# Sigmoid attention and a token-mixing MLP on one core: the whole order of work planned anew, with fixed buffers taken in turn

## The chip, the cores and the metric

The kernel runs on one core of a Trainium2 chip. The metric is the device time of one execution in microseconds (us). A core has five engines that each work through their own list of instructions in order: TensorE (PE in the profile: matmuls; its weight loads are PEld), VectorE (DVE), ScalarE (ACT), GpSimd (POOL) and SyncE (SP, which here only issues DMA transfers). An instruction that waits for a semaphore holds up everything behind it on its own engine.

## What is computed

```python
# q, k, v: (8, 12, 448, 64) float32; 8 sequences, 12 heads
scores = scale * np.matmul(q, k.transpose(0, 1, 3, 2)) - np.log(S)
attn = 1.0 / (1.0 + np.exp(-scores))
attn_out = np.matmul(attn, v)
# x: the heads side by side, (8, 448, 768)
wq = x @ w_q                       # 768 -> 64
wk = x @ w_k                       # 768 -> 64
W_tok = scale * np.einsum('bsd,btd->bst', wq, wk)
mixed = np.einsum('bst,btd->bsd', W_tok, x)
out = np.maximum(mixed, 0.0) @ w_out     # 768 -> 768, float32
```

Matmuls run in bf16. The kernel never forms W_tok: it computes wk-transposed times x first (a 64x768 matrix per sequence, `tmp`) and then wq times that.

## The kernel before

The work is cut into 24 groups of four heads (n = 0 to 23), three to a sequence. For each group the kernel loads q, k and v (448 KB each, `load1`) in float32 on SyncE's queue into eight load buffers, casts them to bf16 (`cast1`), transposes q and k into a tile `qk` (`tr`), and then takes seven steps. Step i of a group computes the scores of 64 keys against all 448 queries for four heads with four 64x64 quarter matmuls (`scores`, L328), turns them through one sigmoid on ScalarE into a tile `at` (L333), and multiplies `at` with v, again four quarter matmuls accumulating over the seven steps (`values`, L350). After the seventh step VectorE copies the sum to `xt` (L359).

How q and k of a group get transposed differs by group and is one letter in the plan. Kinds a and q go through TensorE: matmuls against the identity (L246 or L238) and one or two copies from PSUM on VectorE (L302, L316). Kind c interleaves pairs in the cast (L201); six copies of 32 partitions on GpSimd (`arrange`, L163 to L169) put the blocks in place and two transposes of 128x448 on VectorE (L285) finish it. Kind r ("quadrants") does without GpSimd's copies: two transposes of 128x448 (L278) and four of 32x448 (`quadrants`, L254) on VectorE.

Per sequence the MLP follows: `tr_x` transposes `xt` back to token order `xn`, either as eight whole 128x128 matmuls (L372) or as 32 quarter ones (L388); `mlp_wqk` makes wq and wk (L425, or in quarters L413), `mlp_wkn` transposes wk, `mlp_tmp` makes `tmp`, `mlp_mix` the mixed tokens with a relu into `mx` (L480 on VectorE, L478 on ScalarE), and `out_pair`, `out_halves` and `out_chunk` multiply with w_out and store.

The order of all this is written out by hand as one string, `PLAN` (L134), read one letter at a time by the loop at L828. A letter emits one step (S scores, P values, x or X a transpose of xt, W, N, U, M, O for the MLP; the choice of letter sets the engine of a copy or the tiling). The list `BANKS` (L69) says, one entry for each use, which of the eight PSUM banks it takes. `ORDER` (L705) is the order of the loads and casts: a plain entry is cast on GpSimd, a dot means VectorE, a capital ScalarE. `pump_loads` (L728) issues a load when the buffer eight loads back has been cast; `pump` (L778) emits GpSimd's casts as soon as the tiles that they write are free. Tiles come from rotating pools. Filler letters F and f (L830, L835) emit matmuls on zeros that nothing reads.

Of the kernel before, what the change touches and what calls it, by code (L numbers as in the profile page):

```python
# [17 lines left out]
def kernel(  # L18
# [112 lines left out]
    TW = (1, 2,)  # L131
# [4 lines left out]
        "PSPPPPSSXWzSSwWWSWWXSNSSPPPrSsPPUSPPzSPSPSPCMPPPSPSqkSSMSXSM"
        "SCcPPPSPPxSPdPSOSwwrSSwwWWxSOSSOsOSNPPSPPzCPSPPSIISISIcPSPdP"
        "PSPS2SPPOOSxSUSPPSMPPPcSPPSdOwWwSSMWWWoSMPPSPPPP1SSPcdOQSxSO"
        "OSSNCSOOXcdSSOOSTSPPPSrPPCPSPPCPPSPPPSPSOwowSSSwsOzOxSwwWPSP"
        "MSPPPPRSScSdXXOXoSMSOoNSMPPSPcPPSPPSUdSOSMOSOMoPSPPcPPSPSdPw"  # L140
        "WXWSMSWWWXSSONOScTSOSOSOOdSPOSrOSPPPGPPSPPPSPPsPSPOSPOSOzSQS"
        "XPcPPSPPPSPOSOdSOSxOlLlSLlLPSPPPxPP2GSPOOScOmdOSOOSNO1SQSTPP"
        "PcS1PPSPOPSOSOQSMOSOSOdScOOSdOMSOmOP2PSPPxSPPP12SOSOSOSxOllL"
        "SllcSLPPPSPPPSPOOdSxSOOSOSOSONQSTPSPPPSPPPSPPPxPPmPPLxLlMlGL"
        "lOOyOoNIItIiIMimIiMOoOOOoOoOOOOOOOOOoOO"
# [787 lines left out]
```

## Time and profile before

| | |
|---|---|
| runs, us | 181.77, 180.97, 180.97 (median 180.97) |
| span of the profiled execution, first to last instruction | 180.1 us |
| instructions in it | 7907 |
| busy: TensorE matmul | 169.6 us, 94% |
| busy: VectorE | 145.6 us, 81% |
| busy: ScalarE | 159.0 us, 88% |
| busy: GpSimd | 121.4 us, 67% |
| granted TensorE clock | 1.000 |
| moved by DMA | 47.31 MB, mean 263 GB/s |

Busy shares are averages over the span; the engines wait for each other in different ways at its start, in its middle and after the last sigmoid, so the stages have to be read apart. In a timeline row the first number is the start in us from the span's start, the second the time until the last instruction of the row ends; matmuls are pipelined, so the distance from one start to the next says what one costs. Of a row with a bracket, the bracket is the idle time of the engine ahead of it and what ended it.

### The profile page before, as it was taken

What the parts mean: (1) busy time and instruction counts of PE and PEld (TensorE: products, weight loads), DVE (VectorE), ACT (ScalarE), POOL (GpSimd) and SP (SyncE); (2) the same over time, 40 slices, a digit from 0 to 9 for tenths busy, and PEclk for the clock granted to TensorE, in tenths of its full rate; (3) what the DMA queues carried; (4) which work ended last, traced back from release to release, by engine and by line L of the source; (5) the groups of instructions that cost most, each with busy time, mean ns of one, the idle gap of its engine ahead of it and who ended that gap; (6) DMA issues with size and microseconds to landing.
All of it is one profiled execution on the core that took longest, in us unless ns stands there. A gap on an engine that the chain in (4) does not pass through costs nothing.

```text
span 180.1 us, 7907 instructions
## 1 busy us (share of the span) xinstructions
PE 169.6 (94%) x3440; PEld 112.2 (62%) x3440; DVE 145.6 (81%) x227; ACT 159.0 (88%) x208; POOL 121.4 (67%) x166
## 2 busy tenths in 40 slices
PE   7698899889899999999999999999999999999990
PEld 3334445444575555445667786678887788888660
DVE  3578899997989896889999999979898886768351
ACT  4699999999899999999999999999999989976300
POOL 1028799689999999999999999979979910010000
PEclk9999999999999999999999999999999999999999
DMA  5999999999999998899998889987795523505876
GB/s 177 355 372 349 322 383 381 280 302 356 342 294 349 339 265 267 217 319 365 343 300 315 217 288 305 342 322 213 200 338 173 135 64 73 137 4 122 201 208 175
DMA packets 27475, 47.31 MB, mean 263 GB/s; under 512 B 3888, under 2 KB 23600, under 8 KB 27440
## 3 DMA queue, kind: packets, MB, share of 16 engines
q1 hardware_dynamic: 26160, 44.64, 78.0%
q0 software_dynamic: 800, 1.18, 3.6%
q10 hardware_dynamic: 480, 0.98, 1.5%
q8 instruction: 27, 0.44, 1.0%
q14 instruction: 8, 0.07, 0.1%
HBM read 35.78 MB, written 11.01 MB: 260 GB/s over the span
## 4 chain that ended last, share of the span: by engine, by line
PE 56%; POOL 16%; DMA 15%; DVE 5%; ACT 2%; issue 2%; SPq 1%; POOLq 0%
PE banks L539 15%; PE banks L350 10%; PE banks L328 10%; PE banks L620 8%; DMA q<-in_q_dram 6%; POOL qk L201 5%; DMA w<-in_moe_w_k_dram 4%; DMA k<-in_k_dram 3%; POOL qk L169 3%; DMA wout<-wout 2%; ACT at L333 2%; POOL v L218 2%; PE banks L579 2%; PE banks L413 2%; POOL swap L163 2%
## 5 line engine op out<-in xcount | busy, mean ns | idle before, releaser
L333 ACT ACTIVATE at<-banks 128x896 bf16<-128x896 f32 x168 | 140.0, 948 | 3.4 <-PE banks L328 3.0
L328 PE MATMUL banks<-qk 64*64 64x448 bf16 x672 | 62.2, 358 | 3.3 <-ACT at L333 1.6
L350 PE MATMUL banks<-at,v 64*64 64x448 bf16 x672 | 47.3, 351 | 0.8 <-ACT at L333 0.7
L328 PEld LDWEIGHTS <-qk 64*64 64x64 bf16 x672 | 25.9, 105 | 20.7 <-issue 13.2
L539 PE MATMUL banks<-wout,mx 64*64 64x384 bf16 x672 | 36.6, 323 | 0.0
L201 POOL CAST qk<-k 128x896 bf16<-128x896 f32 x19 | 22.8, 1199 | 10.6 <-DVE qk L302 9.7
L350 PEld LDWEIGHTS <-v 64*64 64x64 bf16 x672 | 23.2, 107 | 8.6 <-issue 1.7
L539 PEld LDWEIGHTS <-mx 64*64 64x64 bf16 x672 | 23.3, 107 | 4.5 <-issue 0.5
L359 DVE CAST xt<-banks 128x896 bf16<-128x896 f32 x22 | 23.8, 1083 | 2.3 <-PE banks L350 1.8
L620 PE MATMUL banks<-wout,mx 128*128 128x384 bf16 (+1 forms) x138 | 24.4, 320 | 0.0
L480 DVE TENSOR_SCALAR mx<-banks 128x1024 bf16<-128x1024 f32 (+3 forms) x22 | 21.3, 972 | 1.9 <-PE banks L493 0.7
L201 POOL CAST qk<-q 128x896 bf16<-128x896 f32 x17 | 20.4, 1198 | 2.6 <-DMA q<-in_q_dram 1.3
L218 POOL CAST v<-v 128x896 bf16<-128x896 f32 x22 | 20.6, 950 | 1.4 <-DMA v<-in_v_dram 0.4
L620 PEld LDWEIGHTS <-mx 128*128 128x128 bf16 x138 | 12.3, 98 | 9.8 <-issue 3.2
L285 DVE STREAM_TRANSPOSE qk<-qk 128x448 f32<-128x448 f32 x28 | 17.0, 627 | 0.4 <-POOL qk L166 0.3
L163 POOL COPY swap<-qk 32x448 uint32<-32x448 uint32 x28 | 15.5, 554 | 2.3 <-DVE qk L201 0.7
L166 POOL COPY qk<-qk 32x448 uint32<-32x448 uint32 x28 | 15.8, 566 | 1.6
L169 POOL COPY qk<-swap 32x448 uint32<-32x448 uint32 x28 | 15.8, 564 | 1.6
L254 DVE STREAM_TRANSPOSE qk<-qk 32x448 f32<-32x448 f32 x24 | 15.3, 636 | 0.6
L422 POOL COPY wq<-wqk 64x448 bf16<-64x448 bf16 x3 | 1.7, 555 | 15.7 <-DVE wqk L421 15.7
L653 DVE COPY o<-banks 128x384 f32<-128x384 f32 x12 | 6.6, 553 | 5.7 <-PE banks L620 5.3
L653 ACT COPY o<-banks 128x384 f32<-128x384 f32 x9 | 4.4, 490 | 7.1 <-PE banks L620 6.9
(91 smaller groups left out, 206.5 us busy)
## 6 DMA issues: line engine op xcount, KB each, us to landing
q<-in_q_dram SPq DMA_DIRECT2D x24, 448.0 KB, 6.6
v<-in_v_dram SPq DMA_DIRECT2D x24, 448.0 KB, 6.3
k<-in_k_dram SPq DMA_DIRECT2D x23, 448.0 KB, 7.0
out_dram<-o SPq DMA_DIRECT2D x50, 192.0 KB, 3.9
wout<-in_moe_w_out_dram POOLq DMA_DIRECT2D x2, 576.0 KB, 12.2
wout<-wout SPq DMA_DIRECT2D x12, 96.0 KB, 6.2
out_dram<-o ACTq DMA_DIRECT2D x4, 192.0 KB, 3.5
k<-in_k_dram SPq DMA_DIRECT2D x1, 256.0 KB, 5.6
```

The lines of the kernel that those rows point to most:

```text
L163: eng.tensor_copy(out=z[lo], in_=w[hi, 0])
L169: eng.tensor_copy(out=w[lo, 1], in_=z[lo])
L201: COPY[e](out=f[:, :, "qk".index(nm)].rearrange("p e i d y -> p e y i d"), in_=ld.pop((nm, n)),)
L218: COPY[e](out=t16.rearrange("p b i d -> p (b i d)"), in_=ld.pop((nm, n)).rearrange("p b x -> p (b x)"),)
L285: nc.vector.transpose(out=qk[n][:, t].rearrange("p t i n -> p (t i n)").bitcast(F32), in_=w)
L328: nc.tensor.matmul(sc[HALF[h], g, 0:S], qk[n][HALF[g], h, 1, i, :], qk[n][HALF[g], h, 0].rearrange("p i n -> p (i n)"), start=True, stop=True,
L333: inst = nc.scalar.activation(at, sc[:, :, 0:S], ACTF.Sigmoid, bias=attn_bias, scale=attn_scale)
L350: nc.tensor.matmul(ps[HALF[g], h, 0:S], ld["v16", n][HALF[h], g, i, :], ats[n, i][HALF[h], g, :], start=(i == 0), stop=(i == NI - 1),)
L359: read(fb, COPY[eng](out=xt(u, j)[:, :, 0:S], in_=ps[:, :, 0:S]))
L480: inst = nc.vector.tensor_scalar(dst, ps, moe_scale, 0.0, ALU.mult, ALU.max)
L539: nc.tensor.matmul(ps[HALF[x], y, 0:NB], mx[HALF[y], u, b, 64 * (i - 3 * y) : 64 * (i - 3 * y) + 64], wout16[HALF[y], slot(y, b), x * NB : ...
L620: nc.tensor.matmul(ps, mxs[w][:, 2 * S * c + m * P : 2 * S * c + (m + 1) * P], wout16[:, c, w0:w1], start=(c == 0), stop=(c == NC - 1),)
```

## The change

The change rewrites the plan, the order of loads and the choice of banks, and replaces the rotating pools by fixed buffers.

- Each entry of `PLAN` now carries its banks ("S23": scores in banks 2 and 3); the `BANKS` list is gone. There are 625 entries in place of 640. The six F and four f fillers are gone.
- `p_ld`, `p_c16`, `p_v16`, `p_qk`, `p_x`, `p_mx` and `p_o` become lists of fixed tiles, in the same numbers, taken in turn (`turn`, or by n modulo the count). A load takes any free buffer of the eight (`borrow`), and one that has been cast goes back to the list; before, the buffers went round in a ring.
- Casts: four are on VectorE (k1, k6, v10, v12) where there were seven (q1, k1, q2, q12, q22, k22, v22), none on ScalarE (v19 before), the others on GpSimd; v6 is loaded and cast in one go by GpSimd's own DMA (L225 after). v0 is now loaded ahead of k2.
- Kinds: five groups in quadrants (3, 4, 5, 8, 18) where there were six (2, 4, 5, 8, 13, 18); TensorE transposes groups 0, 1, 2 and 6 (before 0, 1, 3 and 6); the other 15 (before 14) are of kind c.
- `tr_x`: 18 groups in quarter matmuls and 6 in whole ones (before 14 and 10).
- Some copies change engine. TensorE's list changes its tiling 58 times, the one after the matmuls that warm it up among them (before 68).

The core of the diff (`PLAN` and `ORDER` cut to a line each; other lines that take a pool tile change in the same way as those shown):

```diff
-    p_ld = pool("ld", 8)
-    p_c16 = pool("c16", 2)
-    p_v16 = pool("v16", 4)
-    p_qk = pool("qk", 8)
...
+    lds = [singles.tile([P, 2 * RUN + PAD], F32, name=f"ld{n}") for n in range(8)]
+    v16s = [singles.tile([P, 2, NI, HD], BF16, name=f"v16{n}") for n in range(4)]
+    qks = [singles.tile([P, 2, 2, NI, NP], BF16, name=f"qk{n}") for n in range(8)]
...
+    def turn(nm, bufs):
+        turns[nm] = turns.get(nm, -1) + 1
+        return bufs[turns[nm] % len(bufs)]
+
+    def borrow(key):
+        held[key] = free.pop(0)
+        return held[key]
...
     PLAN = (
-        "ffSSSffKSSF11aSb1SFFrSFSFSSFSqSPPsPPSPzkPSPSPPPSxSrSsPPPPSPPS"
...
+        "S23 S45 K01 1 S67 S01 S23 a45 S01 b S23 S01 S45 S01 S45 q23 S01 p67 P k S45 P P r p R "
...
-        t = p_ld.tile([P, 2, NI * HD], F32, tag="ld", name=nm + "32")
+        t = halves(borrow((nm, n)))
...
-            qk[n] = p_qk.tile([P, 2, 2, NI, NP], BF16, tag="qk", name="qk")
+            qk[n] = qks[n % 8]
...
     ORDER = (
-        ".q1 .k1 k2 .q2 q3 v0 w2 k3 v1 k4 q4 v2 w0 k5 q5 w1 v3 W5 v4 q6 k6 w4 k7 v5 q7 v6 q8 k8 k9 "
...
+        "q1 .k1 v0 k2 q2 q3 k3 v1 k4 q4 v2 w0 v3 q5 v4 k5 w1 q6 w4 v5 .k6 q7 *v6 k7 q8 k8 q9 k9 "
...
-            if len(ring) >= 8 and ring[-8] not in cast:
+            if not free:
                 break
...
         cast.add((nm, n))
+        if (nm, n) in held:
+            free.append(held.pop((nm, n)))
         pump_loads()
...
-    for t in PLAN:
+    for t, b in PLAN:
+        assert not bank
+        if b:
+            bank.append(b)
```

Where the change moves instructions, first on VectorE, early, before the change: from the cast of group 2's q on. Here qk_283 and qk_429 are the casts of groups 2 and 4 that the transposes read, xt_111 to xt_113 the attention sums of groups 0 to 2.

```order
L201 CAST qk_283<-q_169 128x2x2x224
L278 STREAM_TRANSPOSE qk<-qk_283 128x448 x2
L254 STREAM_TRANSPOSE qk<-qk_283 32x448 x4
L316 COPY qk<-banks 128x2x2x448
L359 CAST xt_111<-banks 128x2x448
L401 COPY xn<-banks 128x2x4x128
L278 STREAM_TRANSPOSE qk<-qk_429 128x448 x2
L254 STREAM_TRANSPOSE qk<-qk_429 32x448 x2
L359 CAST xt_112<-banks 128x2x448
L359 CAST xt_113<-banks 128x2x448
L377 COPY xn<-banks 128x4x256
L254 STREAM_TRANSPOSE qk<-qk_429 32x448 x2
```

The same place on VectorE after the change (L290 and L266 are the transposes, L328 the copy of a group that TensorE transposed, L371 the xt cast, L413 and L389 the xn copies). qk_114, qk_115 and qk_116 are the transposed tiles of groups 2, 3 and 4.

```order
L328 COPY qk_114<-banks 128x2x2x448
L290 STREAM_TRANSPOSE qk_115<-qk_120 128x448 x2
L371 CAST xt_90<-banks 128x2x448
L266 STREAM_TRANSPOSE qk_115<-qk_120 32x448 x4
L413 COPY xn_126<-banks 128x2x4x128
L371 CAST xt_91<-banks 128x2x448
L290 STREAM_TRANSPOSE qk_116<-qk_121 128x448 x2
L266 STREAM_TRANSPOSE qk_116<-qk_121 32x448 x2
L371 CAST xt_92<-banks 128x2x448
L389 COPY xn_126<-banks 128x4x256
L266 STREAM_TRANSPOSE qk_116<-qk_121 32x448 x2
```

Group 2 has moved from VectorE's quadrants to TensorE, group 3 the other way. The six transposes that stood ahead of the copy of a TensorE group now stand behind one.

On ScalarE, in the last third, before the change (at is a sigmoid, v16 the bf16 form of v19, mx a relu, o an output copy):

```order
L333 ACTIVATE at4_99<-banks_88 128x896
L218 CAST v16_3054<-v32_2231 128x896
L478 ACTIVATE mx_2640<-banks_88 128x512
L333 ACTIVATE at5_100<-banks_88 128x896
L333 ACTIVATE at6_101<-banks_88 128x896
L478 ACTIVATE mx_2640<-banks_88 128x2x512
L333 ACTIVATE at7_102<-banks_88 128x896
L333 ACTIVATE at8_103<-banks_88 128x896
L333 ACTIVATE at9_104<-banks_88 128x896
L550 COPY o_3230<-banks_88 128x384
L333 ACTIVATE at10_105<-banks_88 128x896
```

The same place on ScalarE after the change (L345 is the sigmoid, L490 the relu):

```order
L345 ACTIVATE at4_78<-banks_67 128x896
L490 ACTIVATE mx0_128<-banks_67 128x512
L345 ACTIVATE at5_79<-banks_67 128x896
L345 ACTIVATE at6_80<-banks_67 128x896
L490 ACTIVATE mx0_128<-banks_67 128x2x512
L345 ACTIVATE at7_81<-banks_67 128x896
L345 ACTIVATE at8_82<-banks_67 128x896
L345 ACTIVATE at9_83<-banks_67 128x896
L345 ACTIVATE at10_84<-banks_67 128x896
```

The cast of v19 and the output copy have left ScalarE; the sigmoids and relus around them stand as before.

More of the change, by code (lines that the diff above doesn't have):

```diff
@@ L90, in bank2 @@
     def bank2():
-        lo, hi = (int(b) for b in BANKS.pop())
+        lo, hi = (int(b) for b in bank.pop())
         take(lo, hi)
@@ L96, in bank1 @@
     def bank1():
-        b = int(BANKS.pop())
+        b = int(bank.pop())
         take(b)
@@ L119, with halves @@
     wq2s = [singles.tile([P, S], BF16, name=f"wq2{n}") for n in range(2)]
+    lds = [singles.tile([P, 2 * RUN + PAD], F32, name=f"ld{n}") for n in range(8)]
+    v16s = [singles.tile([P, 2, NI, HD], BF16, name=f"v16{n}") for n in range(4)]
+    qks = [singles.tile([P, 2, 2, NI, NP], BF16, name=f"qk{n}") for n in range(8)]
+    qk16s = [singles.tile([P, 2, 2, NI, 32, 2], BF16, name=f"qk16{n}") for n in range(2)]
+    t16s = {nm: [singles.tile([P, NI, 2, HD], BF16, name=f"{nm}16{n}") for n in range(2)] for nm in "qk"}
+    xn_bufs = [singles.tile([P, 4, D], BF16, name=f"xn{n}") for n in range(2)]
+    mx_bufs = [singles.tile([P, 2 * 12 * 256], BF16, name=f"mx{n}") for n in range(2)]
+    o_bufs = [singles.tile([P, 2 * NB], F32, name=f"o{n}") for n in range(3)]
+    turns = {}
+    free = list(lds)
+    held = {}
+    def turn(nm, bufs):
[4 more added lines that the diff above has]
+        return held[key]
+    def halves(t):
+        return t[:, 0 : 2 * RUN].rearrange("p (g x) -> p g x", g=2)
     ctx.enter_context(tc.manual_schedule())
@@ L128, in xt @@
         return xts[u % 2 * NJ + j]
-    TW = (1, 2,)
+    TW = (1, 2)
     PLAN = (
-        "ffSSSffKSSF11aSb1SFFrSFSFSSFSqSPPsPPSPzkPSPSPPPSxSrSsPPPPSPPS"
[L136 to L145, printed above, removed]
-    )
-    KIND = ["a"] + [t for t in PLAN if t in "qacer"]
[21 rows of a table added]
+    )
+    PLAN = [(t[0], t[1:]) for t in PLAN.split()]
+    KIND = ["a"] + [t for t, _ in PLAN if t in "qacer"]
     ld = {}
@@ L198, in cast1 @@
             if n not in pq:
-                pq[n] = p_c16.tile([P, 2, 2, NI, 32, 2], BF16, tag="qk16", name="qk16")
+                pq[n] = turn("qk16", qk16s)
             f = pq[n]
@@ L222, in cast1 @@
             return
-        t16 = p_c16.tile([P, NI, 2, HD], BF16, tag=nm + "16", name=nm + "16")
+        t16 = turn(nm, t16s[nm])
         COPY[e](
@@ L365, in tr_x @@
         if j == 0:
-            xns[u] = p_x.tile([P, 4, D], BF16, tag="xn", name="xn")
+            xns[u] = xn_bufs[u % 2]
         if whole:
@@ L546, in out_pair @@
             return
-        o = p_o.tile([P, 2, NB], F32, tag="o", name="o")
+        o = turn("o", o_bufs).rearrange("p (b x) -> p b x", b=2)
         if split:
@@ L569, in out_halves @@
             part = 0
-            ot[0] = p_o.tile([P, 2, NB], F32, tag="o", name="o")
+            ot[0] = turn("o", o_bufs).rearrange("p (b x) -> p b x", b=2)
         o = ot[0]
@@ L614, in out_chunk @@
         if nb == 0 and not part:
-            ot[0] = p_o.tile([P, D], F32, tag="o", name="o")
+            ot[0] = turn("o", o_bufs)
         o = ot[0]
@@ L675 @@
     KA, KB = slice(0, 3), slice(3, 7)
-    q0 = p_ld.tile([P, 2, NI * HD], F32, tag="ld", name="q32")
-    k0 = p_ld.tile([P, 2, NI * HD], F32, tag="ld", name="k32")
+    q0 = halves(borrow(("q", 0)))
+    k0 = halves(borrow(("k", 0)))
     src = {
@@ L791, in cast_next @@
         pump()
-    q016 = p_c16.tile([P, NI, 2, HD], BF16, tag="q16", name="q16")
-    k016 = p_c16.tile([P, NI, 2, HD], BF16, tag="k16", name="k16")
+    q016 = turn("q", t16s["q"])
+    k016 = turn("k", t16s["k"])
     def cast_part(t16, t32, r, e):
@@ L805, with tr_part @@
     cast |= {("q", 0), ("k", 0)}
+    free.append(held.pop(("q", 0)))
     pump_loads()
-    qk[0] = p_qk.tile([P, 2, 2, NI, NP], BF16, tag="qk", name="qk")
-    def tr_part(nm, t16, r, e):
+    qk[0] = qks[0]
+    def tr_part(nm, t16, r, e, b=None):
+        if b:
+            bank.append(b)
         fb, _, ps = bank2()
@@ L815, in tr_part @@
         ))
-    tr_part("q", q016, IA, "v")
-    tr_part("q", q016, IB, "s")
-    tr_part("k", k016, KA, "v")
+    tr_part("q", q016, IA, "v", "01")
+    tr_part("q", q016, IB, "s", "23")
+    tr_part("k", k016, KA, "v", "45")
     cast_part(k016, k0, KB, "v")
+    free.append(held.pop(("k", 0)))
+    pump_loads()
     used |= {("q", 0), ("k", 0)}
@@ L826 @@
     quads_r = []
-    for t in PLAN:
+    for t, b in PLAN:
+        assert not bank
+        if b:
+            bank.append(b)
         if t == "F":
@@ L903 @@
                 pump()
-    assert not chunks and not opened and not BANKS
+    assert not chunks and not opened and not bank
 _INS = ['q', 'k', 'v', 'moe_w_q', 'moe_w_k', 'moe_w_out']
```

21 lines of the change are left out of this document (8 added, 13 removed), and 37 rows, old and new, of tables (BANKS, ORDER, PLAN).

## The prediction

> **What bounds the kernel now.** I read first the busy time of each engine by stages (from:to in us, then the length, then busy us and count for PE, PEld, DVE, ACT and POOL, granted clock, DMA share, GB/s).
>
> ```profile
> 0.00:17.00 17.00, 13.66 (x203) 6.63 (x207) 10.20 (x28) 12.84 (x17) 4.90 (x11) 1.00 0.89 311
> 17.00:36.00 19.00, 17.35 (x359) 9.54 (x354) 17.38 (x25) 19.00 (x25) 16.08 (x19) 1.00 1.08 342
> 36.00:72.00 36.00, 34.75 (x642) 19.96 (x631) 31.60 (x47) 35.18 (x46) 33.14 (x46) 1.00 0.99 314
> 72.00:95.00 23.00, 22.90 (x390) 13.23 (x390) 20.63 (x32) 22.42 (x30) 21.84 (x29) 1.00 0.97 309
> 95.00:157.00 62.00, 62.00 (x1565) 49.08 (x1560) 54.09 (x75) 60.56 (x77) 44.88 (x63) 1.00 0.74 224
> 157.00:180.10 23.10, 18.90 (x340) 13.80 (x332) 11.74 (x24) 9.02 (x19) 0.56 (x1) 1.00 0.53 139
> ```
>
> Three stages. From 17 to 36 us ScalarE (ACT) is busy all 19.00 us: the sigmoids set the pace, VectorE (DVE) fills 17.38 of 19. From 95 to 157 TensorE (PE) is busy 62.00 of 62 and ACT 60.56: both are the limit. After 157 the sigmoids are over and TensorE's last products run alone. Next the timeline of ACT, one row for its whole stretch:
>
> ```profile
> 19.61 21.27 ACT L333 ACTIVATE at<-banks 128x896 bf16<-128x896 f32 x26
> ```
>
> 26 sigmoids in 21.27 us without a gap, 0.82 each. There are 168 of them (24 groups of four heads, 7 each), so a sigmoid that is late before 95 us delays what follows. The first of group n, sigmoid 7n, needs that group's transposed q and k.
>
> So the third view is the timeline of VectorE (start, length, instruction), which makes them:
>
> ```profile
> 20.12 0.69 DVE L401 COPY xn<-banks 128x1024 bf16<-128x1024 bf16 x1 [0.56 <-PE banks L388]
> 20.84 1.17 DVE L278 STREAM_TRANSPOSE qk<-qk 128x448 f32<-128x448 f32 x2
> 22.04 1.28 DVE L254 STREAM_TRANSPOSE qk<-qk 32x448 f32<-32x448 f32 x2
> 23.36 2.12 DVE L359 CAST xt<-banks 128x896 bf16<-128x896 f32 x2
> 25.48 0.69 DVE L377 COPY xn<-banks 128x1024 bf16<-128x1024 bf16 x1
> 26.20 1.28 DVE L254 STREAM_TRANSPOSE qk<-qk 32x448 f32<-32x448 f32 x2
> 27.64 0.62 DVE L430 CAST wqk<-banks 128x448 bf16<-128x448 f32 x1 [0.16 <-PE banks L425]
> 28.18 0.68 DVE L377 COPY xn<-banks 128x1024 bf16<-128x1024 bf16 x1
> 28.78 0.28 DVE L446 COPY wkn<-banks 128x256 bf16<-128x256 bf16 x1
> 29.09 1.17 DVE L278 STREAM_TRANSPOSE qk<-qk 128x448 f32<-128x448 f32 x2
> 30.29 1.28 DVE L254 STREAM_TRANSPOSE qk<-qk 32x448 f32<-32x448 f32 x2
> 31.61 0.56 DVE L458 CAST tmp<-banks 128x384 bf16<-128x384 f32 x1
> 32.08 1.08 DVE L359 CAST xt<-banks 128x896 bf16<-128x896 f32 x1
> 33.20 1.30 DVE L254 STREAM_TRANSPOSE qk<-qk 32x448 f32<-32x448 f32 x2
> ```
>
> The last row ends group 5 at 34.50. TensorE's first score matmuls of group 5:
>
> ```profile
> 34.64 0.38 PE L328 MATMUL banks<-qk 64*64 64x448 bf16 x4
> ```
>
> They start 0.14 us later. In this stage VectorE's list is just in time already; that is the place to watch.
>
> **The early list on VectorE.** Groups 3, 4 and 5 are now the ones made in quadrants (two full transposes and four small ones each); before, they were 2, 4 and 5 there, and group 3 went through TensorE with one copy. Group 3 can't start before its k is loaded and cast. k3 is the ninth block of 448 KB in both load orders. Before, GpSimd cast it when it landed:
>
> ```profile
> 15.74 0.93 POOL L224 CAST k<-k 128x896 bf16<-128x896 f32 x1 [0.35 <-DMA k<-in_k_dram]
> ```
>
> Now this cast has the interleaved form, which the same engine does in
>
> ```profile
> 17.90 1.21 POOL L201 CAST qk<-k 128x896 bf16<-128x896 f32 x1 [0.18 <-DMA k<-in_k_dram]
> ```
>
> so group 3's transposes begin at 15.74 + 1.21 = 16.95, and VectorE, which has had only group 2's copy to do, is idle till then. From there its list to the end of group 4 is two pairs of full transposes, four pairs of small ones, three xt casts, two xn copies. From start to start above: full pair 1.20 (20.84 to 22.04), small pair 1.32, xt cast 1.06, xn copy 0.72. 2.40 + 5.28 + 3.18 + 1.44 = 12.30, end 29.25. For group 5 another xn copy, wqk cast 0.54, full pair 1.20, wkn copy 0.31, two small pairs 2.64, tmp cast 0.47, xt cast 1.06: 6.94, end 36.19. Before it was 34.50, so group 5's scores come at about 36.4 in place of 34.64: **1.8 us late**. Bounds: if k3 lands as much earlier as VectorE's list is late, nothing; if VectorE also idles in this stretch as it does before (19.00 - 17.38 = 1.6), 3.4. I take 1.8, since the list has no slack and the landing has a row. That the third score step now also stands behind k0's second transposes costs some 0.4 at 8 us, which lies inside the 1.8.
>
> **Casts and loads.** Four q/k casts more and one v cast fewer on GpSimd, six 32-partition copies more, and v6 loaded and cast by GpSimd's own DMA: 4 x 1.2 + 6 x 0.56 - 0.95 + 0.84 = 8 us by the rows of these groups on the page. Two q casts, done before 22 us in time that waits for loads, pay about 2 of it. The rest is hidden by GpSimd's lead: its work from 95 to 157 is 44.88 of 62. If that cover were gone it would cost up to 6. v6's DMA stands behind the two wout loads on that queue; the page has
>
> ```profile
> wout<-in_moe_w_out_dram POOLq DMA_DIRECT2D x2, 576.0 KB, 12.2
> ```
>
> It is issued near 33.5, so it lands by some 46 and its first product follows score step 52, near 50: nothing, or 2 us if it queues longer. The buffers in turn and the free list let SyncE's loads go when any buffer is free and not the oldest; loads are paced by 311 to 342 GB/s till 36 us, so I put them at 0 (below, -0.5; above, +1 where a store waits at the head of SyncE's queue).
>
> **ScalarE's other work.** Up to the last sigmoid it loses two 384-column output copies before step 104, and after that one 768-column copy, two 384-column copies and the cast of v19; it gains one 1024-column relu.
>
> ```profile
> 125.06 1.02 ACT L478 ACTIVATE mx<-banks 128x1024 bf16<-128x1024 f32 x1
> 125.96 2.56 ACT L333 ACTIVATE at<-banks 128x896 bf16<-128x896 f32 x3
> 128.40 0.49 ACT L550 COPY o<-banks 128x384 f32<-128x384 f32 x1
> 128.76 4.21 ACT L333 ACTIVATE at<-banks 128x896 bf16<-128x896 f32 x5
> ```
>
> and from the groups of instructions (busy us, mean ns)
>
> ```profile
> L218 ACT CAST v<-v 128x896 bf16<-128x896 f32 x1 | 0.9, 930 | 0.0
> ```
>
> A relu takes 0.90 of its time, a copy 0.36, the 768-column copy taken as two, the cast 0.9. Before step 104: -0.7, and it counts in full, since ACT sets the pace there. After: -0.72 - 0.72 - 0.9 + 0.9 = -1.4; TensorE is full there too, so between 0 and -1.4: I take half, -0.7. What leaves ACT goes to VectorE (three output copies of 0.95 more), which has 8 us free in 95:157, and its six q/k casts and one v cast become two and two.
>
> **TensorE.** Four x transposes change from 8 whole matmuls to 32 quarter ones:
>
> ```profile
> 24.82 0.62 PE L372 MATMUL banks<-ident,xt 128*128 128x128 bf16 x8
> 25.28 0.35 PE L425 MATMUL banks<-xt,wqk 128*128 128x448 bf16 x1
> ...
> 26.73 0.38 PE L328 MATMUL banks<-qk 64*64 64x448 bf16 x4
> 27.05 0.55 PE L425 MATMUL banks<-xt,wqk 128*128 128x448 bf16 x2
> ...
> 44.81 0.45 PE L388 MATMUL banks<-ident,xt 64*64 64x64 bf16 x32
> 45.09 0.36 PE L328 MATMUL banks<-qk 64*64 64x448 bf16 x4
> ```
>
> Whole: 0.46 (24.82 to 25.28). Quarter: 0.28. Gain 0.18 a group. A change of tiling shows as the excess over 0.19 per four quarter matmuls or per full one: 26.73 to 27.05 is 0.32, so 0.13. The order has 58 changes for 68, but most that go lie beside the filler matmuls and early transposes, where ACT sets the pace; after step 104 one group and two changes go: 0.18 + 0.26 = -0.4. The page TensorEngine Tiling (Array Packing) of the Trainium skill, Key Properties, says that a change of mode drains the array; the trace's 0.13 agrees, and all ten changes by that rule would be -1.3 where I count two. The tail after the last sigmoid holds the same matmuls in nearly the same order: 0.
>
> **Sum.** The profiled execution spans 180.1; the median of the runs is 180.97, so 0.9 lies around the span. 180.1 + 1.8 - 0.7 - 0.7 - 0.4 + 0.9 = **181.0 us**, no change (0.5%, 0.9 us, is about what a measurement of this kernel tells from none). Its own range, with 1 either way for the DVE list and 0.7 for ACT: 179.8 to 182.2.
>
> **Rivals.** *Slower: VectorE stays the bound to group 11.* Before, its transposes end at 68.32 and the scores start at 69.62:
>
> ```profile
> 67.16 1.16 DVE L285 STREAM_TRANSPOSE qk<-qk 128x448 f32<-128x448 f32 x2
> ```
>
> ```profile
> 69.62 0.38 PE L328 MATMUL banks<-qk 64*64 64x448 bf16 x4
> ```
>
> From the end of group 5 that is 33.8 us with its waits. The new list there has a v cast and a k cast, an output copy and a net xn copy more and a q cast less, 2.1 us in all. If the waits stay, group 11 ends at 36.2 + 33.8 + 2.1 = 72.1 where 69.62 + 1.8 = 71.4 would be wanted, and the delay is 2.6. It decides as soon as VectorE's waits between 36 and 72 keep over half of their time. With no gain from ACT after 95 us: 180.97 + 2.6 - 0.7 - 0.4 = 182.5; against it, an engine that is behind waits less. Chance 0.26. *Faster: the early list isn't late*, because k3 lands and is cast some 2 us sooner (loads before it are freed sooner), or what is late early on falls into waits of ACT for TensorE that go: then 180.97 - 0.7 - 1.4 - 0.4 = 178.5, or 179.2 with half of ACT's gain. For it: VectorE's whole list is 4 us shorter by the same prices; against it: the landing at 15.74 is paced by the loads ahead. Chance 0.28. *The clock falls.* The six full and eight half filler matmuls between the first scores go; the granted clock is 1.00 over 0:17 with them. TensorE has 13.66 of 17 us busy there, and if a third of it ran at half speed, ACT would be late by up to 3: 184. TensorE: Matmul & The Clock Gate in the Trainium skill, on the HAM clock gate, says that an idle window halves the clock; no row here shows such a gap once the scores run. Chance 0.04.
>
> **How the numbers follow.** Forecast 0.42; slower 0.30; faster 0.28. The cases at 178.5 to 179.2 and at 182.5 to 184 take half each; the range reaches into both: 179.0 to 183.0, leaving a tenth outside on each side.
>
> **What would show it.** Right: in the new trace VectorE runs without idle from about 17 to 36 us, group 5's scores start near 36.4, ACT has gaps of some 1.5 us in all between 28 and 37, and 104 comes within 1 us of the old time. Wrong if ACT shows no gap there (faster), if gaps recur near 72 (slower), or if the stage after 95 us, TensorE full in both, differs by over 1.5 us, for then a wait that I haven't named decides.

## The result, and the profile after

The changed kernel takes 192.59 us (median of 4 runs, 190.32 to 193.14), the kernel before on the same chip 181.37 (180.97 to 183.2). The ratio is 1.056, with a 95% interval of 1.047 to 1.065: slower by 5.6%, outside the forecast range. Medians here are over all runs, ratios and intervals leave out the few that were disturbed.

The profiled execution took 193.14 us, with a span of 191.4. By stages (from:to, length, then busy us and count of PE, PEld, DVE, ACT, POOL, granted clock, DMA share, GB/s):

```profile
0.00:17.00 17.00, 11.21 (x164) 5.68 (x168) 5.34 (x20) 11.75 (x15) 6.23 (x12) 0.87 0.90 324
17.00:36.00 19.00, 16.10 (x318) 9.26 (x311) 17.38 (x27) 17.26 (x22) 16.88 (x21) 0.94 1.05 347
36.00:72.00 36.00, 34.30 (x688) 19.67 (x688) 32.98 (x48) 35.67 (x45) 29.62 (x40) 1.00 0.91 275
72.00:95.00 23.00, 22.85 (x391) 13.84 (x394) 18.58 (x30) 22.32 (x29) 21.50 (x31) 1.00 0.88 276
95.00:157.00 62.00, 56.72 (x1330) 43.01 (x1325) 46.18 (x65) 51.93 (x64) 54.02 (x74) 0.97 0.73 231
```

Two stages are worse. At the start the clock falls to 0.87 and 0.94, and ScalarE, once busy all 19 us of the second stage, has 17.26. Between 95 and 157 TensorE and ScalarE lose 5.3 and 8.6 us, while GpSimd goes from 44.88 to 54.02. The view of waits says the same of the sigmoids (us in total, times, longest), first before, then after:

```profile
ACT at L333 <- PE banks L328: 3.0, 9, 0.7
```

```profile
ACT at L345 <- PE banks L340: 11.4, 21, 2.1
```

The best single reading is the start of each of the 168 sigmoids, from the span's start, beside its start in the profiled execution before. The lateness in us at some score steps, for the changed kernel and for the runs of the next section:

| run | 16 | 40 | 88 | 100 | 108 | 120 | 132 | 136 | 167 |
|---|---|---|---|---|---|---|---|---|---|
| the changed kernel | 2.8 | 3.9 | 2.7 | 3.2 | 7.9 | 8.1 | 8.4 | 10.7 | 11.2 |
| e1, old plan, new buffers | -0.2 | -0.3 | -0.5 | -0.5 | -0.5 | -0.5 | -0.4 | 0.1 | -0.2 |
| e2, old start | -0.4 | -0.4 | -1.6 | -1.2 | 3.5 | 3.6 | 4.0 | 5.5 | 6.3 |
| e3, old rest | 2.6 | 4.0 | 2.9 | 2.9 | 2.9 | 3.6 | 3.6 | 3.6 | 5.2 |
| e4, no block copies from group 13 | 2.2 | 3.6 | 2.5 | 2.8 | 2.9 | 2.9 | 3.5 | 5.3 | 6.1 |
| e5, old plan, no fillers | 1.6 | 1.5 | 0.4 | 0.4 | 0.4 | 0.4 | 0.4 | 0.4 | 0.7 |
| e7, one transpose moved | 2.5 | 3.5 | 2.4 | 2.8 | 3.8 | 7.0 | 7.4 | 8.9 | 9.9 |
| e8, code shifted | 2.5 | 3.5 | 3.5 | 4.0 | 7.3 | 8.1 | 8.5 | 8.6 | 8.5 |
| e9, three letters moved | 2.0 | 3.2 | 2.0 | 2.4 | 3.4 | 6.6 | 7.0 | 7.8 | 8.2 |
| e12, new middle only | -0.1 | -0.2 | -1.5 | 1.0 | 1.0 | 2.6 | 2.7 | 2.7 | 8.1 |
| e13, two casts on VectorE | 1.8 | 3.1 | 3.0 | 3.4 | 4.2 | 5.0 | 5.4 | 7.1 | 7.6 |
| e14, all mends | 1.9 | 3.4 | 3.3 | 3.7 | 3.8 | 5.3 | 5.7 | 5.8 | 5.7 |
| e15, old plan, more GpSimd work | -0.1 | 0.8 | 5.7 | 5.7 | 5.7 | 5.7 | 5.7 | 5.7 | 6.4 |

Of the 11.2 us, most is lost in four places: by step 16 (2.8, or 3.0 from step 0), by step 40 (1.1), between 100 and 108 (4.7), and between 132 and 136 (2.3). From 40 to 88 a gain of 1.2 stands against them, and 1.5 more are lost in small pieces, some 0.5 each from 88 to 100, from 108 to 132 and behind 136. After the last sigmoid nothing is added (the spans differ by 11.3).

**The start.** VectorE after the change, from group 2's copy on:

```profile
18.16 1.09 DVE L328 COPY qk<-banks 128x1792 bf16<-128x1792 bf16 x1 [4.88 <-PE banks L250]
19.17 1.16 DVE L290 STREAM_TRANSPOSE qk<-qk 128x448 f32<-128x448 f32 x2
...
36.94 1.30 DVE L266 STREAM_TRANSPOSE qk<-qk 32x448 f32<-32x448 f32 x2
```

Group 3's transposes begin at 19.17, not at 16.95: they stand behind group 2's copy in VectorE's list, and that copy waited 4.88 us for TensorE. Group 5 ends at 38.24 (before 34.50). TensorE had been late since its first wait:

```profile
8.40 0.32 PE L250 MATMUL banks<-ident,k 64*64 64x64 bf16 x16 [2.02 <-DVE k L811]
...
17.48 0.63 PE L250 MATMUL banks<-ident,k 64*64 64x64 bf16 x27
```

The third score step is queued behind the matmuls at 8.40, and group 2's k (17.48) behind a score step and two value steps. From 9.23 to 12.64 and from 16.05 to 19.47 us all this runs at half clock besides.

**Steps 100 to 108.** GpSimd, VectorE and TensorE around group 16's first transpose:

```profile
98.42 2.31 POOL L213 CAST qk<-ld 128x896 bf16<-128x896 f32 x2
100.80 1.17 POOL L175 COPY swap<-qk 32x448 uint32<-32x448 uint32 x2
102.02 1.17 POOL L178 COPY qk<-qk 32x448 uint32<-32x448 uint32 x2
```

```profile
100.00 0.63 DVE L297 STREAM_TRANSPOSE qk<-qk 128x448 f32<-128x448 f32 x1
103.22 0.65 DVE L297 STREAM_TRANSPOSE qk<-qk 128x448 f32<-128x448 f32 x1 [2.59 <-POOL qk L178]
103.79 0.92 DVE L564 COPY o<-banks 128x768 f32<-128x768 f32 x1
```

```profile
102.04 0.58 PE L362 MATMUL banks<-at,v 64*64 64x448 bf16 x8
104.76 0.59 PE L340 MATMUL banks<-qk 64*64 64x448 bf16 x4 [2.15 <-DVE o L564]
```

This is a chain over three engines. GpSimd's casts and copies run without a gap and end at 103.19. VectorE stands 2.59 us at a transpose whose scores are due only ten steps later, with an output copy queued behind it. The copy holds two PSUM banks, and TensorE's next score step needs them. And the wait has a sequel, in the granted clock (first number after POOL's):

```profile
101.00:104.80 3.80, 1.65 (x40) 1.10 (x32) 1.58 (x3) 2.31 (x3) 3.44 (x7) 1.00 0.44 147
104.80:108.20 3.40, 3.40 (x31) 1.83 (x30) 2.13 (x3) 1.11 (x2) 3.22 (x5) 0.50 0.59 127
108.20:111.60 3.40, 3.40 (x73) 2.41 (x69) 3.12 (x5) 3.09 (x4) 3.16 (x5) 1.00 0.75 263
```

For 3.4 us TensorE is busy throughout and gets 31 matmuls done, in the next 3.4 us 73.

**Steps 132 to 136.** TensorE in the middle of the products of one value tile:

```profile
130.16 0.73 PE L362 MATMUL banks<-at,v 64*64 64x448 bf16 x9
132.80 0.38 PE L362 MATMUL banks<-at,v 64*64 64x448 bf16 x3 [1.91 <-issue]
```

A releaser "issue" means that the profile shows nothing that it waited for.

### The profile page after: what moved, and what is told of

Read it like the earlier page. It is cut to its first block, busy times and chain, and to the rows that moved or that the text cites. A ratio compares the mean times of both kernels' runs of the same rounds, so it can differ in the third digit from the quotient of the medians.

```text
span 191.4 us, 8061 instructions
## 1 busy us (share of the span) xinstructions
PE 171.3 (90%) x3522; PEld 114.7 (60%) x3522; DVE 139.5 (73%) x221; ACT 159.8 (84%) x205; POOL 129.4 (68%) x176
## 4 chain that ended last, share of the span: by engine, by line
PE 60%; DVE 15%; DMA 9%; ACT 5%; POOL 4%; issue 3%; SPq 1%; POOLq 0%
PE banks L340 13%; PE banks L362 11%; PE banks L632 11%; PE banks L551 10%; DMA ld<-in_q_dram 6%; ACT at L345 5%; DVE qk L266 5%; DVE xt L371 4%; PE banks L437 3%; PE banks L591 3%; PE banks L400 2%; DMA out_dram<-o 2%; PE banks L425 2%; PE banks L481 1%; DVE qk L290 1%
## 5 line engine op out<-in xcount | busy, mean ns | idle before, releaser
L345 ACT ACTIVATE at<-banks 128x896 bf16<-128x896 f32 x168 | 141.3, 930 | 11.9 <-PE banks L340 11.4
L340 PE MATMUL banks<-qk 64*64 64x448 bf16 x672 | 65.5, 366 | 9.2 <-ACT at L345 3.7
L213 POOL CAST qk<-ld 128x896 bf16<-128x896 f32 x40 | 46.7, 1197 | 9.6 <-DVE qk L297 5.1
L362 PE MATMUL banks<-at,v 64*64 64x448 bf16 x672 | 48.8, 357 | 1.9 <-issue 1.9
L340 PEld LDWEIGHTS <-qk 64*64 64x64 bf16 x672 | 27.5, 107 | 29.0 <-issue 21.1
L371 DVE CAST xt<-banks 128x896 bf16<-128x896 f32 x22 | 23.9, 1086 | 4.5 <-PE banks L362 3.9
L297 DVE STREAM_TRANSPOSE qk<-qk 128x448 f32<-128x448 f32 x30 | 18.7, 633 | 3.6 <-POOL qk L178 3.0
L230 POOL CAST v<-ld 128x896 bf16<-128x896 f32 x21 | 19.3, 931 | 2.5 <-DMA ld<-in_v_dram 2.0
L413 DVE COPY xn<-banks 128x1024 bf16<-128x1024 bf16 (+1 forms) x18 | 11.5, 637 | 2.6 <-PE banks L400 2.0
L266 DVE STREAM_TRANSPOSE qk<-qk 32x448 f32<-32x448 f32 x20 | 12.7, 636 | 0.4
L564 DVE COPY o<-banks 128x768 f32<-128x768 f32 x11 | 10.4, 947 | 3.2 <-ACT at L345 2.6
L490 ACT ACTIVATE mx<-banks 128x448 bf16<-128x448 f32 (+2 forms) x11 | 7.4, 686 | 3.6 <-PE banks L505 2.8
(80 smaller groups left out, 182.6 us busy)
## 6 DMA issues: line engine op xcount, KB each, us to landing
wout<-in_moe_w_out_dram POOLq DMA_DIRECT2D x2, 576.0 KB, 12.6
```

The source lines that it names most:

```text
L213: COPY[e](out=f[:, :, "qk".index(nm)].rearrange("p e i d y -> p e y i d"), in_=ld.pop((nm, n)),)
L230: COPY[e](out=t16.rearrange("p b i d -> p (b i d)"), in_=ld.pop((nm, n)).rearrange("p b x -> p (b x)"),)
L266: nc.vector.transpose(out=qk[n][other : other + 32, h].rearrange("p t i n -> p (t i n)").bitcast(F32), in_=w[own : own + 32, 1 - h],)
L297: nc.vector.transpose(out=qk[n][:, t].rearrange("p t i n -> p (t i n)").bitcast(F32), in_=w)
L340: nc.tensor.matmul(sc[HALF[h], g, 0:S], qk[n][HALF[g], h, 1, i, :], qk[n][HALF[g], h, 0].rearrange("p i n -> p (i n)"), start=True, stop=True,
L345: inst = nc.scalar.activation(at, sc[:, :, 0:S], ACTF.Sigmoid, bias=attn_bias, scale=attn_scale)
```

## Experiments

All kernels below are timed in three rounds against the kernel before on the same chip (medians of it from 181.14 to 182.18 us). PLAN entries are quoted as the kernel writes them.

**e1 to e3: which part of the change costs?** e1 puts the old PLAN, BANKS and ORDER on the new buffers; e2 takes the first 40 score steps and their loads from the old plan, e3 the first 40 from the new one.

```diff
# e1
-    PLAN, ORDER: new
+    PLAN, ORDER: old, each letter with its old bank
# e2
+    PLAN = old[:step 40] + new[step 40:]
# e3
+    PLAN = new[:step 40] + old[step 40:]
```

> The kernel after with the plan, the banks and the order of loads and casts of before: only the fixed buffers in turn and the free list are new. Theory (the loss lies in the new order): the time of before, 180.5 to 182. Rival (fixed buffers or the free list cost time by themselves): 184 or more, up to the 192 of after.

> The kernel after with the first 40 score steps, their fillers, loads and casts planned as before, and the rest of the new plan. In the trace of after the sigmoids are 3.8 us late by step 40 and lose 7.4 more between steps 104 and 140. Theory (two separate losses, the second from GpSimd being late in the new rest): 192.6 - 3.8 = 188.5 to 189.5. Rival (the late loss is the start's lateness carried on): 181 to 183.

> The reverse: the new plan for the first 40 score steps, the plan of before from there on. Theory: 181 + 3.8 = 184.5 to 185.5. Rival (the start's lateness is given back by the slack of the rest): 181 to 182.5.

e1: 181.86 us, ratio 1.003 (0.998 to 1.007). The fixed buffers and the free list cost nothing that can be measured. e2: 187.99, 1.036 (1.030 to 1.043). e3: 185.46, 1.024 (1.016 to 1.032). The two parts of the plan lose 3.6% and 2.4%, together 6.0%, where the whole loses 5.6%: start and rest are separate losses.

**e4: GpSimd's block copies left out from group 13 on.** The transposes then read tiles whose blocks are not in place, so the output of these groups differs; the order of everything else is kept.

```diff
-        if KIND[n] in "er":
+        if KIND[n] in "er" or n >= 13:
             return
```

> The kernel after without GpSimd's six block copies for the groups from 13 on (ten groups, 37 us of GpSimd's work; q and k of these groups stay in unsorted blocks). Theory (GpSimd's lateness holds VectorE's queue and with it TensorE's banks): the losses after step 104 go, 192.6 - 7 = 184.5 to 186.5. Rival (bank order or ScalarE's order causes them): within 1.5 us of 192.6.

187.71 us, 1.034 (1.026 to 1.041). GpSimd's work between 59 and 104 us (fifth busy column), first before, then here:

```profile
59.00:104.00 45.00, 44.90 (x768) 26.97 (x760) 40.11 (x58) 43.68 (x57) 42.28 (x59) 1.00 0.92 293
```

```profile
59.00:104.00 45.00, 44.81 (x785) 26.67 (x784) 38.83 (x56) 43.88 (x56) 33.12 (x41) 1.00 0.86 280
```

With some 9 us less on GpSimd, steps 100 to 108 lose 0.1 us in place of 4.7, and nothing else in that stretch was changed. The first row says something else that the prediction should have seen: the kernel before has GpSimd busy 42.28 of 45 us there. The changed kernel has 41.99, no more: GpSimd was full already, and what it got in addition is done later, in the 54.02 of 62 us behind 95. The losses at the start and at 132 stay.

**e15: the same question put to the kernel before.** Two copies that nothing reads are added on GpSimd behind the block copies of five groups.

```diff
             eng.tensor_copy(out=w[lo, 1], in_=z[lo])
+        if 9 <= n < 15:
+            for g in range(2):
+                eng.tensor_copy(out=gdst[0:32], in_=gsrc[0:32])
```

> The kernel before's plan with two copies of 32 partitions more on GpSimd behind the block copies of groups 9 to 12 and 14, which nothing reads: 10 copies of some 0.6 us, 6 us of work that nobody waits for by itself. Theory (GpSimd is full from 59 to 97 us and its lead over the scores is 1.3 to 4 us): transposes come late for groups 12 to 16 and the time rises by 1.5 to 4 us, 183 to 186. Rival, the prediction's own reading (GpSimd has 17 us free between 95 and 157 and the work is hidden): within 0.7 us of 181.6.

187.86 us, 1.037 (1.030 to 1.045). The group of the added copies, and TensorE where they land:

```profile
L187 POOL COPY gdst<-gsrc 32x448 uint32<-32x448 uint32 x10 | 5.5, 550 | 0.6
```

```profile
78.59 0.76 PE L368 MATMUL banks<-at,v 64*64 64x448 bf16 x12 [3.63 <-POOL v L236]
```

The v cast that it waited for, in the kernel before and here, with the fourth pair of added copies ahead of it:

```profile
73.28 0.93 POOL L218 CAST v<-v 128x896 bf16<-128x896 f32 x1
```

```profile
75.41 1.16 POOL L187 COPY gdst<-gsrc 32x448 uint32<-32x448 uint32 x2
77.61 0.92 POOL L236 CAST v<-ld 128x896 bf16<-128x896 f32 x1
```

Eight of the ten copies were done by then, 4.4 us of work that nobody waits for. The cast comes 4.3 us later, and the sigmoid of step 82 is 4.3 us late. The half-clock interval that follows the wait (from 79.46 us) brings this to 5.6 by step 84. The last two copies, at 88.3 us, cost nothing more: the lateness stays at 5.7 until step 140. So up to here work added to GpSimd shows in the sigmoids in full: it has no lead, in the old order either. The first to be late was not a transpose, as the theory had it, but a v cast queued behind the copies.

**e13: two casts back on VectorE** (q12 and q13), the order of transposes and copies as in the change.

```diff
-    ORDER ... .v10 W5 q12 k12 ... q13
+    ORDER ... .q12 .v10 W5 k12 ... .q13      # and a "1" behind "d" of groups 10 and 11
```

> The changed kernel with the casts of q12 and q13 on VectorE in place of GpSimd; the order of transposes and copies stays as it is. Theory (GpSimd has no lead from 59 to 104 us): GpSimd's list there is 2.3 us shorter, so at group 16's first transpose VectorE waits under 1 us in place of 2.59, TensorE's wait for the output copy (2.15 us) falls to under 0.8, no half-clock interval follows, and steps 100 to 108 lose 1 to 2 us in place of 4.7: 189 to 190. Rival (only the order costs): two casts more on VectorE bring its copies later and nothing is gained: 192 to 193.

189.13 us, 1.044 (1.034 to 1.053). The same place on VectorE and TensorE:

```profile
100.86 0.65 DVE L298 STREAM_TRANSPOSE qk<-qk 128x448 f32<-128x448 f32 x1 [0.92 <-POOL qk L179]
101.43 0.92 DVE L565 COPY o<-banks 128x768 f32<-128x768 f32 x1
```

```profile
102.40 0.38 PE L341 MATMUL banks<-qk 64*64 64x448 bf16 x4 [0.48 <-DVE o L565]
```

The wait shrinks from 2.59 to 0.92, TensorE's from 2.15 to 0.48, no half-clock interval follows, and steps 100 to 108 lose 0.8 us. Between 68 and 80, where the two casts now stand on VectorE, it loses 1.6 us, the change only 0.5.

**e7 and e9: the order on VectorE.** e7 moves one letter: c, group 16's first transpose, behind the output copy. e9 moves its second transpose too, and at the start k of group 2 directly behind q.

```diff
# e7, e9
-    S01 O d c S67 O P01 m23 O S67
+    S01 O d S67 O P01 m23 O c S67
# e9
-    R p R d p S23 R P S45
+    R p R p S23 R P d S45
-    q23 S01 p67 P k S45
+    q23 k S01 p67 P S45
```

> The changed kernel with one letter moved: group 16's first transpose, which needs GpSimd's copies and is wanted only at score step 112, stands behind the next output copy in VectorE's list and not ahead of it. Theory (the order in VectorE's queue, then a bank, then the clock): the copy is done near 101.6 us in place of 104.7, TensorE's wait of 2.15 us for it goes, the clock doesn't fall at 104.8, and of the 4.7 us lost between steps 100 and 108 about 3.5 to 4.5 come back: 188.1 to 189.1. Rival (GpSimd is simply short of time there, whatever the order): group 16's or 17's transposes are late by their own scores and the loss comes back by step 120; under 1.5 us gained, 191 or more.

> The changed kernel with three letters moved: k of group 2 directly behind its q on TensorE, not behind a score step and two value steps; group 16's first transpose behind the next output copy, as before; its second transpose behind the next attention-sum copy as well. Theory (places in the queues): the wait of TensorE for VectorE's attention-sum copy, 1.87 us in the run with one letter moved, goes too, and steps 100 to 112 lose under 1 us in place of 4.8 (3.0 with one letter); the copy of group 2 ends a microsecond sooner and of the 2.4 to 2.8 us lost by step 16 some 0.7 to 1.2 come back. The stalls in the instruction stream (1 to 2.3 us) stay somewhere. 192.6 - 4 - 1 = 187.6, 186.6 to 188.6 us. Rival (GpSimd is short of time): group 16's later second transpose makes step 112 late, the loss only moves to 112 to 120: 190 or more.

e7: 191.43 us, 1.050 (1.040 to 1.061); e9: 190.25, 1.049 (1.042 to 1.056). In e7 the loss from 100 to 108 falls from 4.7 to 1.0, and the wait for the output copy is gone, but by step 120 the lateness is 7.0 again: TensorE meets the next one.

```profile
105.73 0.30 PE L506 MATMUL banks<-wqk,tmp 64*64 64x256 bf16 x2 [1.87 <-DVE xt L372]
```

The transposes still come when GpSimd lets them. e9, with that one moved as well, arrives at step 120 with 6.6. So both theories had a half: the order decides where GpSimd's lateness strikes and how dear it is (with or without the clock), but most of it comes back somewhere. Less work on GpSimd takes it away: all of it in e4, most of it in e13. k of group 2 moved ahead brought 0.5 us by step 16 against e7, below the 0.7 to 1.2 expected.

**e5, e6 and e10: the fillers and the clock of the start.** e5 takes the old plan's fillers out, e6 puts thirteen into the new one, e10 puts eight where TensorE waits for k0.

```diff
# e5: old plan
-    ffSSSffKSSF11aSb1SFFrSF...
+    SSSKSS11aSb1SrS...
# e6
-    S23 S45 K01 1 S67 S01 S23 a45 ...
+    F2 S23 S45 K01 1 F6 S67 F0 S01 S23 a45 ...
# e10
+    S23 S45 F6 F7 F6 F7 F6 F7 F6 F7 K01 1 S67 ...
```

> The kernel before's plan with its ten filler matmul letters taken out, nothing else. Theory (the fillers hold the clock): with fewer matmuls between the first scores the granted clock falls to half for one or two stretches of 3.4 us before 20 us, as it did in the changed kernel (9.2 and 16.1 us), and the sigmoids of steps 8 to 16 come 0.5 to 1.5 us later: 181.7 to 182.7 us beside 181.1. Rival (the start is lost by the order alone): the clock stays at 1.00 or its fall lies in TensorE's waits, the sigmoids come at their old times, 181.1 or a few tenths less.

> The changed kernel with thirteen filler matmuls of 512 columns put back ahead of eleven of its score steps from 0 to 14. Theory (clock): the granted clock stays at 1.00 from some 6 us on, of the 2.8 us that were lost by step 16 about 1 to 1.5 come back, and the time falls from 192.6 to about 191.3. Rival (order: group 2 made on TensorE behind four queued steps): the start stays 2.5 us late with the clock at 1.00, and the time stays within 0.4 of 192.6, or rises by the fillers' own 0.2 us each where TensorE is what is waited for.

> The changed kernel with eight filler matmuls of 512 columns put where TensorE waits 2.0 us for k0's second half (ahead of its transposes), none elsewhere. Theory (the wait at 6.4 to 8.4 us is what halves the clock from 9.2): the clock stays at 1.00 over 9 to 13 us, and of the loss by step 16 some 0.5 to 1 us comes back: about 191.9. Rival (the clock of the first 20 us doesn't hang on this wait, or costs nothing since ScalarE waits for loads): half-clock stretches stay, or go without gain; 192.3 to 193.

e5: 182.6 us, 1.006 (1.001 to 1.011). Its first stage:

```profile
0.00:17.00 17.00, 12.76 (x172) 6.17 (x176) 10.21 (x28) 12.93 (x17) 4.14 (x10) 0.75 0.90 317
```

Without fillers the clock falls to 0.75 there, and the sigmoids lose 2.1 us between steps 4 and 16, but only 0.6% is left at the end. e6: 192.63, 1.056 (1.046 to 1.066); e10: 192.07, 1.056 (1.045 to 1.067). Fillers bring the new plan nothing back. But those of e6 didn't hold the clock: it was at one half from 7.3 to 14.2 us all the same. In e10 the clock is 1.00 from 9.6 to 16.4 us, and the sigmoids still lose 1.2 us between steps 4 and 16, where the kernels with the new start and a lower clock lose 2.1 to 3.0. The clock has a share in the start then, and the order has another, but the two runs don't fix the shares, since fillers also push the first scores back (e10 is 2.2 us late by step 4).

**e8 and e11: the instruction stream.** The 14 warm-up matmuls are cut into 64 with the same columns, which puts everything behind them some 100 instructions later in TensorE's code; e8 does so to the new plan, e11 to the old.

```diff
-    for w in [P] * 8 + [4 * P] * 6:
+    for w in [64] * 64:
```

> The changed kernel with its 14 warm-up matmuls cut into 64 of 64 columns each (the same columns in all), so that all later instructions of TensorE stand some 100 places further in its instruction stream; nothing else changes. Theory (TensorE's instructions ran dry in the dense stretch at 130.9 us because of where the 256-instruction fetches fell): the wait of 1.9 us without a releaser goes, shrinks or moves by some us, and the time falls by up to 2.3 to 190.3, or stays if a fetch then falls badly elsewhere. Rival (something in the plan itself, a semaphore that the trace doesn't show): TensorE waits 1.9 us at the same matmuls and the time stays at 192.6.

> Control for the shifted code: the kernel before's plan with the 14 warm-up matmuls cut into 64, some 100 instructions more ahead of everything. Theory: TensorE's stretches of quarter matmuls are shorter here, so no stall of over 0.5 us without a releaser appears, and the time stays at the plan's 181.1 to 181.9 us. Rival (any plan can stall where a fetch falls badly): a stall of 1 to 2 us without a releaser appears somewhere and the time rises to 182.5 to 183.5.

e8: 191.5 us, 1.044 (1.031 to 1.057). At the old place TensorE now runs through, and a stall without a releaser stands 86 us earlier:

```profile
44.18 0.38 PE L401 MATMUL banks<-ident,xt 64*64 64x64 bf16 x23
45.49 0.26 PE L401 MATMUL banks<-ident,xt 64*64 64x64 bf16 x9 [0.93 <-issue]
...
130.19 0.76 PE L363 MATMUL banks<-at,v 64*64 64x448 bf16 x12
```

Steps 132 to 136 lose 0.1 us in place of 2.3, steps 40 to 48 1.2 more. No data and no order were changed, which leaves TensorE's own instructions as what it waited for. By the times alone no gain is shown, since the intervals of the two ratios overlap. The trace bears the cause out: 27 DMA packets of 16 KB on the queue of instructions feed 7044 instructions, 261 each; between the packets that start at 124.47 and 130.51 TensorE executes 374, and at 130.9 it stops. A count says it more sharply. In all 18 traces TensorE has 23 waits of over 0.15 us without a releaser behind the first 9 us, none of them in the kernel before. I counted the matmuls and weight loads that start ahead of each: 4543 in the changed kernel and in e2, 1471 in e8, 5055 in e3. Divided by 256, all 23 counts leave 190 or 191. Neither chance nor the plan's semaphores, which stand elsewhere in each kernel, would do that; and 256 is about what one packet feeds. This stall, that of e8 and one in e2 (0.7 us) stand in or just behind a transpose in 32 quarter matmuls, which issues 64 instructions in a quarter of a microsecond; others (1.1 us in e2, 1.0 in e3) stand in long runs of the output product's quarter matmuls. e11: 183.11 us, 1.004 (0.999 to 1.010), its longest wait of this kind on a matmul 0.4 us: the old plan, with four such transposes fewer, is hardly touched (the longest in e15 is 0.7 us). That these transposes are what brings the long stalls is argued from where the stalls stand; no run takes the four of them back alone.

**e14: all mends at once**: score step 2 ahead of K01, fillers back, k of group 2 behind q, the two transposes of group 16 moved, q12 and q13 cast on VectorE.

```diff
-    S23 S45 K01 1 S67 S01 S23 a45 S01 b S23 ...
+    f0 f1 S23 S45 S67 f2 f3 K01 F2 1 S01 S23 a45 F0 S01 b S23 ...
     # and the edits of e9 and e13
```

> The changed kernel with all mends at once: score step 2 ahead of k0's second transposes and filler matmuls back at the places of the kernel before, k of group 2 behind its q, group 16's transposes behind the copies, q12 and q13 cast on VectorE. Theory (the named losses are the whole loss): the start is under 1 us late by step 16, steps 96 to 112 lose under 1 us, the early list keeps its 1.1 us, and the instruction stream costs 0 to 2 us: 183 to 185 us. Rival (a part of the loss has another cause): 187 or more, with a loss at a step that isn't named yet.

188.43 us, 1.039 (1.030 to 1.048). From step 88 to 112 it loses 0.5 us in place of 5.4, and from 132 to 136 0.1: these two causes are closed. 1.9 us of the start stay, with eight score matmuls at 9 us taking 0.96 us, as long as at half clock in the changed kernel's 9.2 to 12.6. Four of them take 0.59 us up to 12.6 and 0.38 from 13.5 on: the fillers at these places did not hold the clock, though the view says 1.00 there. The trace's first entry of the clock is at 13.24 us, and ahead of it the 1.00 is no measurement. Of the early list 1.5 stay, and 1.4 between 116 and 120, which the theory had not named and where TensorE waits for GpSimd twice more (0.30 for a v cast, 0.64 for a copy of wq). By its time the rival is right: a part of the loss had not been named.

**e12 and e16: a version to beat both?** The new plan's middle (steps 40 to 94) between the ends of the old one; e16 also casts q12 and q13 on VectorE and keeps the old late loads.

```diff
+    PLAN = old[:step 40] + new[step 40:step 95] + old[step 95:]
```

> The plan of before for score steps 0 to 39 and from 95 on, the changed plan for steps 40 to 94 between them, with the loads in the order that goes with each, on the fixed buffers. Theory (the new plan loses only at its start and after step 96, and gains in the middle): the middle brings the 1.0 to 1.65 us that it showed by step 88 behind the old start, and nothing is lost at the seams: 179.6 us, 179.0 to 180.2. Rival (the middle's gain was only lateness made good, or the new loads of the middle leave groups 14 to 16 late): 181 to 183.

> The kernel with the old ends and the changed middle once more, with q12 and q13 cast on VectorE and with the loads from q16 on in the order of before. Theory (its 8 us were GpSimd's lateness at the seams): the waits of VectorE for GpSimd (2.65 and 2.83 us at 129 and 143) go, and the time is 180 to 182 us, the middle's gain of some 0.5 to 1 us included or eaten. Rival (13 groups in blocks and one in quadrants less is more than GpSimd can do behind the seam whatever the casts): still 184 or more.

e12: 189.77 us, 1.047 (1.038 to 1.057), though its clock is 1.00 throughout. The middle gives 1.2 us between steps 40 and 88 (e1: 0.3, e5: 1.1), and 9.6 are lost behind it, most dearly here:

```profile
129.69 0.65 DVE L298 STREAM_TRANSPOSE qk<-qk 128x448 f32<-128x448 f32 x1 [2.65 <-POOL qk L179]
```

```profile
132.45 0.22 PE L453 MATMUL banks<-ident,wqk 64*64 64x64 bf16 x3 [3.04 <-DVE o L565]
```

That is the chain of steps 100 to 108 at another place, since group 13 is made with GpSimd's copies here too. e16: 186.63, 1.028 (1.022 to 1.035). VectorE's waits for GpSimd fall to 0.73 and less, 3.3 us stay: 2.2 between steps 92 and 96, where TensorE waits 1.7 us for sigmoids at the seam, and 1.2 at 136 to 140. No version was found that beats the kernel before.

## Why the prediction was wrong

**Casts and loads: the failed step.** "The rest is hidden by GpSimd's lead: its work from 95 to 157 is 44.88 of 62." The lead was read from a stage after the one in which it is used up. The row for 72 to 95, quoted in the same prediction, has GpSimd busy 21.84 of 23, and between 59 and 104 it is 42.28 of 45. In e15 4.4 us of added GpSimd work put the sigmoids 4.3 us back; in e4 some 9 us less on it remove the loss. The sentence behind it, "If that cover were gone it would cost up to 6", had nearly the size, steps 100 to 108 cost 4.7, but that is in part luck. What it lacked was the path: not late scores, but an output copy queued behind a transpose, a PSUM bank, and the clock.

**The early list.** That VectorE's list for groups 3 to 5 has no slack was right, and its price nearly so: 1.1 us between steps 16 and 40 (1.4 in e3, 1.5 in e14) for a forecast of 1.8. But the list did not start at 16.95. "VectorE, which has had only group 2's copy to do, is idle till then" took that copy as done; it came at 18.16, and the list stands behind it.

**The start.** "That the third score step now also stands behind k0's second transposes costs some 0.4 at 8 us, which lies inside the 1.8": it cost 1.5 by step 8, and with group 2's way through TensorE 2.8 by step 16, in addition to the early list and not inside it. A loss ahead of a list that has no slack is added to it. The q casts that were to "pay about 2 of it" in time that waits for loads come later, since v0's load now stands ahead of group 2's: GpSimd cast q2 at 14.15, as soon as it had landed, where VectorE did at 12.07 before. But TensorE didn't wait for it: it took q2 at 15.79, 0.7 us after the cast had ended, and its wait just ahead of that was for ScalarE.

**The clock.** The rival had its chance of 0.04 for the fillers. Half-clock intervals came (0.87 and 0.94 in the first two stages), but fillers put back bring nothing (e6, e10), and without them the old plan loses 0.6% (e5). That doesn't clear the clock: in e6 and e14 the fillers didn't hold it, and e5 lost 2.1 us between steps 4 and 16 of which it got 1.2 back by step 88. The prediction's "no row here shows such a gap once the scores run" did not ask what a new wait would do to the clock: the interval at 104.8 belongs to the wait ahead of it.

**TensorE and ScalarE.** The relief in the middle (0.7 us forecast) is 1.2 us between steps 40 and 88, but the old plan on the new buffers shows 0.3 to 1.1 there (e1, e5 and e11), so no more than some tenths can be put down to it. The gains of 0.4 and 0.7 behind step 104 can't be seen: nothing is gained there in any run. The quarter transposes were priced by their duration alone (0.28 for 0.46); that they bring 64 instructions where whole ones bring 16 was left out, and just behind one of them TensorE's code ran dry, which cost 2.3 us. This wait had no term and no rival; the prediction's last sentence named its sign, a difference of over 1.5 us in the stage after 95 for "a wait that I haven't named".

**Right:** the buffers in turn and the free list at 0 (e1), the tail at 0, and the size of GpSimd's additional work: 8 us were forecast, and its busy time went from 121.4 to 129.4. The slower rival (VectorE the bound to group 11, 182.5) did not happen: from step 40 to 88 the lateness falls.

What stays open is how the 2.8 us of the start divide between order and clock, and what holds e16 back at its seam.

## What to carry to other kernels

Read an engine's lead in the stretch where it is spent, not over a longer stage: an engine busy 42 of 45 us there has none, whatever its average says. For an instruction that waits on another engine, ask what stands behind it in its own queue and which buffer that holds; such a wait costs more than the lateness of its own result. And price an exchange of few large instructions for many small ones by their number too, where the engine's instructions are fetched while it runs.
